# Loading half of chunk 0's w from another queue, r.(u k) of a third unit on TensorE, and a new order of all work, in a fused linear-attention and feed-forward kernel

## The chip, the cores and the metric

The kernel runs on one NeuronCore of a Trainium2 chip. The core has five engines with an instruction stream each: TensorE (PE in the profile) for matmuls and transposes, VectorE (DVE), ScalarE (ACT), GpSimd (POOL) and SyncE (SP), which here only issues transfers. Each engine works through its own instructions in order, and they wait for one another by semaphores. Transfers (DMA) are issued by SP and by GpSimd. The metric is the device time of one execution in microseconds (us), lower is better.

## What is computed

Two stages. The first is a linear attention with a decaying state, for 4 batches, 8 heads, 768 steps and head size 48; the second takes its output as 3072 tokens of 384 values through a feed-forward layer in which two products are multiplied.

```python
for t in range(S):
    kt, vt, rt, wt = (k[:, :, t], v[:, :, t], r[:, :, t], w[:, :, t])
    cur = np.einsum('bhd,bhe->bhde', u[None] * kt, vt)
    y[:, :, t] = np.einsum('bhd,bhde->bhe', rt, state + cur)
    state = wt[:, :, :, None] * state + np.einsum('bhd,bhe->bhde', kt, vt)
...
a = x @ w1            # x: 3072 x 384, w1 and w2: 384 x 1024
b = x @ w2
h = a * b @ w3        # w3: 1024 x 1024
return (h @ w_out).astype(np.float32)
```

All inputs and the output are float32.

## The kernel before

**Attention, by units.** The 768 steps are cut into six chunks of 128. A unit is one chunk of one or two batches; `UNITS` lists 13: unit 0 is chunk 0 of batch 0, unit 1 chunk 0 of batch 1, unit 2 chunk 0 of batches 2 and 3, and then two units of two batches for each of chunks 1 to 5. Within a unit (function `unit`, suffix `_t` on every name below) the recurrence is turned into matrix products: `ln` takes the logarithm of w (ACT, L670); `cs` and `ct` are its cumulative sums, in both layouts (TensorE, L679, L686); `ne` and `e` exponentiate them (ACT, L693, L699); `Kt` is k times the inverse decay (DVE, L704); `trr`/`RT` and `trk`/`KT` bring r and the decayed k into the transposed layout (TensorE L768 and L787, then DVE L773, and DVE or ACT L792); `m` is the product of both, `msk` its copy under the causal mask (DVE L812, or ACT L815 followed by a mask pass `maff` on GpSimd, L818); `y` multiplies by v (L850), `ys` adds the state's part (L841); `kv`, `T`, `S`, `Sc`, `Sb` bring the state on.

**The u term.** For each token and head it needs the number r.(u k), `dg`, which then multiplies v (`dv`, L750) and is added to y (`yb`, L862). It comes in one of two ways. Usually DVE or GpSimd multiplies r by k (`rk`, L709) and by u spread over all rows (`ruk`, L744), and DVE sums each head (`dg`, L748). For the units in `PE_DIAG`, TensorE sums: r k is transposed (`rkt`, L722), copied (`rke`, L727) and multiplied by `u_blk` (`d`, L736), a matrix with u in the rows of each head, and the result is copied (`dcp`, L741). `u_blk` is made once: two tiny matmuls from u (`ub`, L549 and L551), a DVE copy (`ublk`, L560) and two selects on GpSimd (`ublk2`, L564 and L566). `yt`/`xT` (L879, L884) transpose y for the second stage; units 9 to 12 do their transposes by DMA from SP.

**Feed-forward, by blocks.** `BLOCKS` joins units 0, 1 and 2 as blocks of their own, then two units each. Function `block` multiplies x by w1 and w2, some columns at a time (`a`, `b`, L939; b_0_1 is the second step of block 0, and steps 0 and 1 of blocks 0 and 1 need the first and second halves of the weights), copies a (`asb`, ACT L948), multiplies a by b (`abT`, DVE L952), and multiplies by `w34` (`o`, L961), which is w3 @ w_out, computed once in the kernel (`wt`, `wm`, L628 to L645). `osb` (L969) copies and SP stores.

**Loads.** Function `load` brings r, k, v and w of a unit (`rin`, `kin`, `vin`, `win`); r, k and v are cast to bfloat16 on the way, w stays float32. The loads in `SP_LOADS` are issued by SP, all others, the weights by `wload` too, by GpSimd.

**What sets the order.** Every piece of work is an `op` with an engine, an estimated duration and a key. The key is a base from the code, plus `RANK` of its kind, plus `STEP` of its name; where an op may run on two engines, `ENGINE` names the one. `schedule` plays the whole program through at build time with these estimates: whenever an engine is free it takes, among the ops that are ready by then, the one with the lowest key. The order so found is written out as each engine's instruction stream; on the chip nothing is chosen anew. An argument `late` makes the planner hold an op until others have ended, with no wait on the chip. Loads have keys near -10000, most other work between 59000 and 130000, so a load that the planner's model of the DMA queue lets through (`AHEAD`) goes ahead of GpSimd's other work.

Of the kernel before, what the change touches and what calls it, by code (L numbers as in the profile page):

```python
# [27 lines left out]
    "table": 113606.5, "ones": 79240, "LT": -1.5, "I128": 5.5, "pads": 139162.5, "rpads": 121276, "state0": 169505.5,  # L28
    "mask": 100743.5, "u": 3, "ub": 60310, "ubc": 114602.5, "ublk": 130965, "ublk2": 130038.5, "w1_0": -5,
    "w2_0": -3, "w1_1": -1, "w2_1": -13.5, "wo": -1, "w3_0": -4, "w3_1": -2, "w3_2": -1, "w3_3": -1, "gate": 23665.5,  # L30
    "wt_0": 171055.5, "w3Te_0": 170507.5, "wm_0": 33207, "w34e_0": 176250, "wt_1": 168598.5, "w3Te_1": 167528,
    "wm_1": 6037.5, "w34e_1": 178855, "wt_2": 170905, "w3Te_2": 175099, "wm_2": 5773.5, "w34e_2": 178246.5,
    "wt_3": 198481.5, "w3Te_3": 175459, "wm_3": 5604.5, "w34e_3": 178230, "wt_4": 198331.5, "w3Te_4": 174917.5,
    "wm_4": 32121, "w34e_4": 176157, "wt_5": 198774.5, "w3Te_5": 169927.5, "wm_5": 32634.5, "w34e_5": 178205.5,
    "wt_6": 198344, "w3Te_6": 176915, "wm_6": 5902.5, "w34e_6": 174984.5, "wt_7": 198309.5, "w3Te_7": 176726.5,
    "wm_7": 32627, "w34e_7": 178641.5, "rpad3": 113432.5, "win_0": 16, "kin_0": 2, "rin_0": 1, "vin_0": 3,
    "ln_0": 26693.5, "cs_0": 124632.5, "ct_0": 58880.5, "ne_0": 138927, "e_0": 171254, "Kt_0": 241553, "rk_0": 34358,
    "ruk_0": 85983, "dg_0": 5362.5, "dv_0": 114281, "trr_0": 155793, "RT_0": 111791.5, "trk_0": 127611,
    "KT_0": 146707.5, "m_0_0": 111506, "msk_0_0": 186441, "maff_0_0": 257875, "y_0": 144830.5, "yb_0": 253063,
# [135 lines left out]
BLOCKS = [[0], [1], [2], [3, 4], [5, 6], [7, 8], [9, 10], [11, 12]]
# [876 lines left out]
```

## Time and profile before

| what | value |
|---|---|
| median of 7 runs | 174.08 us (173.08 to 175.93) |
| the profiled execution | 173.16 us |
| its span, first to last instruction | 171.4 us |
| granted TensorE clock | 0.998 |
| TensorE busy | 153.9 us (90% of the span) |
| DVE, ACT, GpSimd busy | 120.5, 97.8, 108.7 us |
| bytes moved by DMA | 24.12 MB |

The durations in the views come from the one profiled execution; the 1.8 us between its time and its span lie before the first and after the last instruction. In a group of instructions the name of an output stands ahead of an arrow and its inputs behind it; after the count come busy time, mean duration in ns, and the engine's idle time just before these instructions with what ended it. A row of a stretch gives for each engine the busy time and, in brackets, the number of instructions. A row of a DMA issue ends with the size and the us from issue to landing. A row of waits names who waited, for whom, the total, the count and the longest.

### The profile page before, as it was taken

The page shows a single profiled execution, that of the slowest core. Times are in us where ns is not written, and L with a number is a line of the kernel's source. Part 1 is how long each engine was busy: PE and PEld are TensorE (multiplying, and loading weights), DVE is VectorE, ACT ScalarE, POOL GpSimd, SP SyncE. Part 2 cuts the span into 40 slices and gives each one's busy share as a digit, 9 for nine tenths or more (in the row PEclk, how much of TensorE's full clock was granted, in tenths as well). Part 3 has the DMA queues.
Part 4 walks back from the last instruction along what each step waited for, and adds up shares of the span by engine and source line. Part 5 has one row for each costly group of instructions (what it writes and reads, how often), then busy time and mean ns, then how long its engine had stood idle before and what let it go on. Part 6 is the DMA issues. An engine that isn't in the chain of part 4 may idle for free.

```text
span 171.4 us, 4130 instructions
## 1 busy us (share of the span) xinstructions
PE 153.9 (90%) x1711; PEld 98.6 (58%) x1726; DVE 120.5 (70%) x160; ACT 97.8 (57%) x130; POOL 108.7 (63%) x93
## 2 busy tenths in 40 slices
PE   0308799999999999999999999999999999999992
PEld 0206689998676765555756556655645455555560
DVE  5027888989888699999699697977976464231540
ACT  4512549887623785567987847875575643335101
POOL 7979698859799799999999969664142250000000
PEclk9999999999999999999999999999999999999999
DMA  6999999999989999999999998296145222211133
GB/s 102 143 161 183 175 244 172 163 206 173 208 196 142 189 165 137 191 216 144 162 169 257 203 100 155 76 145 181 28 90 100 96 46 48 96 46 46 46 111 121
DMA packets 98315, 24.12 MB, mean 141 GB/s; under 512 B 90680, under 2 KB 96312, under 8 KB 98296
## 3 DMA queue, kind: packets, MB, share of 16 engines
q0 software_dynamic: 78912, 15.47, 108.0%
q1 hardware_dynamic: 19384, 8.39, 21.1%
q8 instruction: 13, 0.21, 0.5%
q14 instruction: 6, 0.05, 0.1%
HBM read 27.79 MB, written 4.72 MB: 190 GB/s over the span
## 4 chain that ended last, share of the span: by engine, by line
PE 84%; DMA 4%; POOL 4%; DVE 3%; issue 2%; ACT 1%; POOLq 0%; ACTq 0%
PE banks L939 36%; PE banks L961 17%; PE banks L640 6%; DMA u_row<-in_u_dram 4%; PE banks L806 4%; PE banks L850 3%; PE banks L686 3%; PE banks L768 2%; PE banks L679 2%; PE banks L628 2%; PE banks L896 2%; PE banks L841 2%; PE banks L787 2%; PE banks L879 1%; POOL rin L580 1%
## 5 line engine op out<-in xcount | busy, mean ns | idle before, releaser
L939 PE MATMUL banks<-xT,w_bf 128*128 128x512 bf16 (+2 forms) x369 | 68.0, 326 | 1.0 <-ACT xT L884 0.3
L939 PEld LDWEIGHTS <-w_bf 128*128 128x128 bf16 x384 | 33.0, 99 | 24.7 <-issue 0.3
L952 DVE TENSOR_TENSOR abT<-a_sb,banks 128x1024 bf16<-128x1024 f32 (+1 forms) x28 | 29.8, 1066 | 19.4 <-PE banks L939 17.8
L948 ACT COPY a_sb<-banks 128x1024 f32<-128x1024 f32 (+1 forms) x28 | 25.0, 893 | 17.2 <-PE banks L939 15.0
L961 PE MATMUL banks<-w,abT 128*128 128x384 bf16 x192 | 34.3, 326 | 0.1
L818 POOL TENSOR_SCALAR_AFFINE_SELECT Mbf<-Mbf 128x1024 bf16<-128x1024 bf16 x16 | 17.4, 1094 | 13.1 <-ACT Mbf L815 13.1
L961 PEld LDWEIGHTS <-abT 128*128 128x128 bf16 x192 | 18.3, 98 | 12.4
L815 ACT CAST Mbf<-banks 128x1024 bf16<-128x1024 f32 x16 | 16.0, 1016 | 5.5 <-PE banks L806 5.5
L969 ACT COPY osb<-banks 128x384 f32<-128x384 f32 x14 | 6.7, 480 | 18.7 <-PE banks L961 18.6
L750 POOL TENSOR_TENSOR dv<-vin,dg 128x768 bf16<-128x768 bf16 (+1 forms) x9 | 12.6, 1406 | 7.1 <-DMA xT<-dv 3.7
L699 ACT ACTIVATE eT<-banks 128x1024 f32<-128x1024 f32 (+1 forms) x13 | 12.4, 957 | 5.7 <-PE banks L686 4.1
L704 DVE TENSOR_TENSOR Kt<-kin,banks 128x768 bf16<-128x768 bf16 (+1 forms) x11 | 9.5, 874 | 8.1 <-DMA kin<-in_k_dram 8.1
L862 DVE TENSOR_TENSOR dv<-banks,dv 128x768 bf16<-128x768 f32 (+1 forms) x13 | 11.6, 891 | 3.5 <-PE banks L850 3.2
L812 DVE TENSOR_TENSOR Mbf<-banks,mask 128x1024 bf16<-128x1024 f32 x8 | 9.8, 1220 | 3.8 <-PE banks L806 3.8
L686 PE MATMUL banks<-LT,lw 128*128 128x128 bf16 x96 | 8.3, 234 | 4.4 <-ACT lw L670 4.4
L709 POOL TENSOR_TENSOR rk<-rin,kin 128x768 bf16<-128x768 bf16 x6 | 9.8, 1641 | 2.5 <-DMA kin<-in_k_dram 2.5
L640 PE MATMUL banks<-wo_bf,w3T 128*128 128x384 bf16 x64 | 11.4, 327 | 0.0
L773 DVE TENSOR_TENSOR KRT<-banks,eT 128x1024 bf16<-128x1024 bf16 (+1 forms) x9 | 9.9, 1103 | 2.0 <-ACT eT L699 1.3
L670 ACT ACTIVATE lw<-win 128x768 bf16<-128x768 f32 (+1 forms) x11 | 8.6, 788 | 4.7 <-DMA win<-in_w_dram 4.4
L693 ACT ACTIVATE banks<-banks 128x768 f32<-128x768 f32 (+1 forms) x13 | 9.8, 752 | 2.4 <-PE banks L679 1.9
L787 PE MATMUL banks<-I,Kt 128*128 128x128 bf16 x64 | 5.0, 231 | 6.6 <-DVE Kt L704 6.6
L580 POOL DMA_DIRECT2D rin<-in_r_dram x7 | 10.0, 1423 | 1.0 <-POOLq L1036 0.8
(91 smaller groups left out, 239.6 us busy)
## 6 DMA issues: line engine op xcount, KB each, us to landing
out_dram<-osb SPq DMA_DIRECT2D x24, 192.0 KB, 2.2
win<-in_w_dram POOLq DMA_DIRECT2D x4, 768.0 KB, 9.2
w_bf<-in_moe_w_dram POOLq DMA_DIRECT2D x4, 512.0 KB, 9.9
w_bf<-in_moe_w_dram POOLq DMA_DIRECT2D x4, 384.0 KB, 7.8
rin<-in_r_dram POOLq DMA_DIRECT2D x4, 384.0 KB, 8.8
kin<-in_k_dram POOLq DMA_DIRECT2D x4, 384.0 KB, 8.6
vin<-in_v_dram POOLq DMA_DIRECT2D x4, 384.0 KB, 8.8
wo_bf<-in_moe_w_out_dram POOLq DMA_DIRECT2D x1, 768.0 KB, 9.5
```

What stands on the lines that cost most here:

```text
L580: op(eng, 60 if eng == "SP" else 650 + 270 * nb, lambda: e.dma_start(dst[:, b0 * H:(b0 + nb) * H, :D], ap), late=SP_ROWS if src == "w" and ...
L640: nc.tensor.matmul(o[:, :DM], lhsT=w3T[fi % 2][:, gi, :], rhs=wo_bf[:, gi, :], start=(gi == 0), stop=(gi == FI - 1))
L686: nc.tensor.matmul(o[:, b, q, :], lhsT=LW[:, b * H + 2 * q:b * H + 2 * q + 2, :].rearrange("t h d -> t (h d)"), rhs=LT, start=True, stop=True)
L699: nc.scalar.activation(ET[:, :, 1:], o[:, :nb * HP, :], Act.Exp)
L750: op("POOL", {"POOL": 100 + 1.8 * N, "DVE": dve(N)}, lambda e: ENG[e].tensor_mul(dvs, vv, dgs[:, :, None].to_broadcast([C, bh, D])), r=[f" ...
L815: nc.scalar.copy(Mbf[m].rearrange("s j q t -> s j (q t)"), banks[:, g.at(MM):g.at(MM) + 2, :])
L818: nc.gpsimd.affine_select(Mbf[m].rearrange("s j q t -> s (j q) t"), Mbf[m].rearrange("s j q t -> s (j q) t"), compare_op=Alu.is_gt, fill=0 ...
L862: nc.vector.tensor_add(ybs.rearrange("t b (q e d) -> t e (b q) d", e=2, d=D), o, dvs.rearrange("t (b q e) d -> t e (b q) d", b=nb, e=2))
L939: nc.tensor.matmul(o[:, q * T // TB, q % (TB // T), :], lhsT=wt[:, di, fi * P:(fi + 1) * P], rhs=xT[x][:, di, :T], start=(di == 0), stop=( ...
L948: nc.scalar.copy(a_sb[sa][:, :nbk * TB], banks[:, g.at(A):g.at(A) + nbk, :].rearrange("p k t -> p (k t)"))
L952: nc.vector.tensor_mul(abT[x][:, f[0]:f[0] + G, :T].rearrange("p i t -> p (i t)"), a_sb[sa][:, :nbk * TB], banks[:, g.at(Bk):g.at(Bk) + nb ...
L961: nc.tensor.matmul(banks[:, g.at(O), :DM], lhsT=abT[x][:, fi, tt * P:(tt + 1) * P], rhs=w34[:, fi, :], start=(fi == 0), stop=(fi == FI - 1))
```

## The change

`SP_LOADS` loses w of unit 2: SP issues w of units 0 and 1 (half of chunk 0's w), GpSimd that of unit 2. `PE_DIAG` gains unit 0. `RANK`, `STEP` and `ENGINE` are new throughout. The constants `WP` and `W3P` are written out as 2 and 4. The table lines below are those for the names that the prediction speaks of; nearly all other entries of the three tables are new as well.

```diff
RANK = {
...
-    "KT": -32021, "Kt": -126599, "RT": 12283, "S": 8478, "Sb": 24178, "Sc": 4497, "T": -63912, "a": -33006,
...
-    "dtk": 4456, "dtr": -30331, "dty": -11348, "dv": 2309, "e": -53690, "gate": -5921, "kv": -22477, "ln": 90720,
-    "m": -52126, "maff": -142053, "mask": 14517, "msk": -62096, "ne": -21947, "o": 72528, "ones": 38044,
...
-    "ubc": 2921, "ublk": -6276, "w34e": -51349, "w3Te": -50030, "wm": 55638, "wt": -109673, "xT": -151029,
...
+    "KT": -59002, "Kt": -156396, "RT": -9537, "S": 9698, "Sb": 4105, "Sc": -1961, "T": -74202, "a": -28563,
...
+    "dtk": 11195, "dtr": -35356, "dty": -11734, "dv": 8664, "e": -47925, "gate": -16883, "kv": -19093, "ln": 89439,
+    "m": -49493, "maff": -142402, "mask": 6933, "msk": -38393, "ne": -23481, "o": 80856, "ones": 46697,
...
}

STEP = {
-    "mask": 100743.5, "u": 3, "ub": 60310, "ubc": 114602.5, "ublk": 130965, "ublk2": 130038.5, "w1_0": -5,
-    "w2_0": -3, "w1_1": -1, "w2_1": -13.5, "wo": -1, "w3_0": -4, "w3_1": -2, "w3_2": -1, "w3_3": -1, "gate": 23665.5,
...
-    "wm_7": 32627, "w34e_7": 178641.5, "rpad3": 113432.5, "win_0": 16, "kin_0": 2, "rin_0": 1, "vin_0": 3,
...
-    "ruk_0": 85983, "dg_0": 5362.5, "dv_0": 114281, "trr_0": 155793, "RT_0": 111791.5, "trk_0": 127611,
...
-    "yt_0": 193451, "xT_0": 268468.5, "kv_0": 85387.5, "T_0": 178871.5, "S_0": 115755, "Sc_0": 117251.5,
...
-    "asb_0_1": 138945.5, "abT_0_1": 267085, "o_0_0": 16544.5, "osb_0_0": 176180, "store_0_0": 3021, "win_1": 5,
...
-    "abT_1_1": 266966.5, "o_1_0": 19075.5, "osb_1_0": 176211.5, "store_1_0": 6906, "win_2": 16, "kin_2": 3,
...
-    "Kt_2": 241604.5, "rk_2": 43019.5, "rkt_2": 123889, "rke_2": 155874, "d_2": 125422, "dcp_2": 43850,
-    "dv_2": 121048, "trr_2": 155377.5, "RT_2": 104841, "trk_2": 127526, "KT_2": 153183, "m_2_0": 112598,
-    "msk_2_0": 179172, "maff_2_0": 265178.5, "m_2_1": 111295.5, "msk_2_1": 179165.5, "maff_2_1": 265358.5,
...
+    "mask": 114325.5, "u": 6, "ub": 85613, "ubc": 115778.5, "ublk": 139994.5, "ublk2": 139582.5, "w1_0": -1,
+    "w2_0": -9, "w2_1": 1, "w3_0": -2, "w3_1": -1, "gate": 18300.5, "wt_0": 186936.5, "w3Te_0": 180388.5,
...
+    "rpad3": 110949.5, "win_0": 9, "kin_0": 2, "rin_0": 1, "vin_0": 7, "ln_0": 30931, "cs_0": 150610.5,
...
+    "rke_0": 160559, "d_0": 138446.5, "dcp_0": 35270, "dv_0": 113183, "trr_0": 168163.5, "RT_0": 130924.5,
...
+    "yb_0": 262883.5, "yt_0": 197545, "xT_0": 274692.5, "kv_0": 92018.5, "T_0": 197296, "S_0": 111557.5,
...
+    "store_0_0": 6002.5, "win_1": -4, "kin_1": -5, "rin_1": 3, "vin_1": 5, "ln_1": 30947, "cs_1": 150772,
...
+    "asb_1_1": 159555.5, "abT_1_1": 287058, "o_1_0": 5697.5, "osb_1_0": 183614.5, "store_1_0": 6383, "win_2": -2,
+    "kin_2": -10, "rin_2": -9, "vin_2": 4, "ln_2": 27502, "cs_2": 150899, "ct_2": 77090, "ne_2": 140677,
+    "e_2": 165156, "Kt_2": 277775, "rk_2": 8720.5, "rkt_2": 141179, "rke_2": 159467, "d_2": 138283.5, "dcp_2": 42304,
+    "dv_2": 112314.5, "trr_2": 168851, "RT_2": 128671.5, "trk_2": 151531.5, "KT_2": 175478, "m_2_0": 122874.5,
+    "msk_2_0": 157605, "maff_2_0": 263855, "m_2_1": 122898.5, "msk_2_1": 162959.5, "maff_2_1": 263536,
...
}

ENGINE = {
...
-    "w34e_5": "ACT", "w3Te_6": "ACT", "w34e_6": "DVE", "w3Te_7": "DVE", "w34e_7": "ACT", "rk_0": "DVE",
-    "ruk_0": "DVE", "dv_0": "DVE", "KT_0": "DVE", "msk_0_0": "DVE", "xT_0": "ACT", "S_0": "POOL", "osb_0_0": "DVE",
...
-    "msk_4_1": "DVE", "xT_4": "DVE", "S_4": "DVE", "osb_3_0": "DVE", "osb_3_1": "DVE", "osb_3_2": "ACT",
-    "osb_3_3": "ACT", "rk_5": "POOL", "ruk_5": "DVE", "dv_5": "DVE", "KT_5": "ACT", "msk_5_0": "ACT",
-    "msk_5_1": "ACT", "xT_5": "ACT", "S_5": "POOL", "rk_6": "DVE", "ruk_6": "POOL", "dv_6": "POOL", "KT_6": "DVE",
-    "msk_6_0": "ACT", "msk_6_1": "ACT", "xT_6": "ACT", "S_6": "POOL", "osb_4_0": "DVE", "osb_4_1": "DVE",
-    "osb_4_2": "ACT", "osb_4_3": "DVE", "rk_7": "DVE", "ruk_7": "DVE", "dv_7": "DVE", "KT_7": "ACT",
-    "msk_7_0": "ACT", "msk_7_1": "ACT", "xT_7": "ACT", "S_7": "POOL", "rk_8": "DVE", "ruk_8": "POOL", "dv_8": "POOL",
-    "KT_8": "ACT", "msk_8_0": "ACT", "msk_8_1": "DVE", "xT_8": "ACT", "S_8": "POOL", "osb_5_0": "ACT",
-    "osb_5_1": "ACT", "osb_5_2": "ACT", "osb_5_3": "ACT", "rk_9": "DVE", "ruk_9": "POOL", "dv_9": "POOL",
-    "msk_9_0": "DVE", "msk_9_1": "ACT", "Sb_9": "DVE", "rk_10": "DVE", "ruk_10": "DVE", "dv_10": "POOL",
...
+    "w34e_5": "DVE", "w3Te_6": "DVE", "w34e_6": "DVE", "w3Te_7": "ACT", "w34e_7": "ACT", "rk_0": "DVE",
+    "rke_0": "DVE", "dcp_0": "ACT", "dv_0": "DVE", "KT_0": "ACT", "msk_0_0": "DVE", "xT_0": "DVE", "S_0": "DVE",
+    "osb_0_0": "ACT", "rk_1": "DVE", "rke_1": "DVE", "dcp_1": "DVE", "dv_1": "POOL", "KT_1": "ACT", "msk_1_0": "DVE",
...
+    "msk_4_0": "ACT", "msk_4_1": "ACT", "xT_4": "ACT", "S_4": "DVE", "osb_3_0": "ACT", "osb_3_1": "ACT",
+    "osb_3_2": "DVE", "osb_3_3": "ACT", "rk_5": "POOL", "ruk_5": "DVE", "dv_5": "POOL", "KT_5": "DVE",
+    "msk_5_0": "DVE", "msk_5_1": "ACT", "xT_5": "ACT", "S_5": "POOL", "rk_6": "DVE", "ruk_6": "DVE", "dv_6": "POOL",
+    "KT_6": "ACT", "msk_6_0": "ACT", "msk_6_1": "DVE", "xT_6": "DVE", "S_6": "POOL", "osb_4_0": "ACT",
+    "osb_4_1": "ACT", "osb_4_2": "ACT", "osb_4_3": "DVE", "rk_7": "DVE", "ruk_7": "DVE", "dv_7": "POOL",
+    "KT_7": "ACT", "msk_7_0": "ACT", "msk_7_1": "ACT", "xT_7": "DVE", "S_7": "DVE", "rk_8": "DVE", "ruk_8": "POOL",
+    "dv_8": "DVE", "KT_8": "ACT", "msk_8_0": "ACT", "msk_8_1": "DVE", "xT_8": "ACT", "S_8": "DVE", "osb_5_0": "ACT",
+    "osb_5_1": "ACT", "osb_5_2": "ACT", "osb_5_3": "ACT", "rk_9": "POOL", "ruk_9": "DVE", "dv_9": "POOL",
+    "msk_9_0": "ACT", "msk_9_1": "ACT", "Sb_9": "POOL", "rk_10": "POOL", "ruk_10": "POOL", "dv_10": "POOL",
...
}
...
@@ -166,15 +167,13 @@
 DMA_KR = set(range(9, 13))
 DMA_Y = set(range(9, 13))
 DMA_R = set(range(9, 13))
-PE_DIAG = {1, 2}
+PE_DIAG = {0, 1, 2}
 
 WARM, FILL = 0.0, 0.0
 
-WP, W3P = 2, 4
-
 BLOCKS = [[0], [1], [2], [3, 4], [5, 6], [7, 8], [9, 10], [11, 12]]
 
-SP_LOADS = {("w", 0), ("w", 1), ("w", 2)}
+SP_LOADS = {("w", 0), ("w", 1)}
 
 CAPS = {"f": 4, "q": 6, "o": 2}
 
@@ -590,15 +589,15 @@
     w1r = moe_w1.rearrange("(di dp) f -> dp di f", dp=P)
     w2r = moe_w2.rearrange("(di dp) f -> dp di f", dp=P)
     wor = moe_w_out.rearrange("(gi gp) o -> gp gi o", gp=P)
-    FH, FQ = DFF // WP, FI // W3P
-    for h in range(WP):
+    FH, FQ = DFF // 2, FI // 4
+    for h in range(2):
         f = slice(h * FH, (h + 1) * FH)
-        wload(w1_bf[:, :, f], w1r[:, :, f], f"w1_{h}", DM * DFF * 4 // WP)
-        wload(w2_bf[:, :, f], w2r[:, :, f], f"w2_{h}", DM * DFF * 4 // WP)
+        wload(w1_bf[:, :, f], w1r[:, :, f], f"w1_{h}", DM * DFF * 2)
+        wload(w2_bf[:, :, f], w2r[:, :, f], f"w2_{h}", DM * DFF * 2)
     wload(wo_bf, wor, "wo", DFF * DM * 4)
-    for h in range(W3P):
+    for h in range(4):
         f = slice(h * FQ, (h + 1) * FQ)
-        wload(w3_bf[:, f, :], w3r[:, f, :], f"w3_{h}", DFF * DFF * 4 // W3P)
+        wload(w3_bf[:, f, :], w3r[:, f, :], f"w3_{h}", DFF * DFF)
 
 
     turn, done = [], 0
@@ -620,7 +619,7 @@
     def w34_block(fi):
         pr = 250 + fi * 12
         T = g.bank(f"wt{fi}", 1, "s")
-        src = f"w3_{fi * W3P // FI}"
+        src = f"w3_{fi // 2}"
 
         def tr():
             o = banks[:, g.at(T), :].bitcast(BF).rearrange("p (g f) -> p g f", f=P)
@@ -939,9 +938,9 @@
                         nc.tensor.matmul(o[:, q * T // TB, q % (TB // T), :], lhsT=wt[:, di, fi * P:(fi + 1) * P],
                                          rhs=xT[x][:, di, :T], start=(di == 0), stop=(di == DI - 1))
             cost = mm(*[T] * (DI * G))
-            op("PE", cost, lambda K=A, f=fis: fill(K, w1_bf, f), r=xs + free + [f"w1_{fis[0] * WP // FI}"],
+            op("PE", cost, lambda K=A, f=fis: fill(K, w1_bf, f), r=xs + free + [f"w1_{fis[0] // 4}"],
                w=[A, f"ad{n}_{z}", f"a_sb{sa}"], prio=pr + fis[0], name=f"a_{n}_{z}")
-            op("PE", cost, lambda K=Bk, f=fis: fill(K, w2_bf, f), r=xs + free + [f"w2_{fis[0] * WP // FI}", f"ad{n}_{z}"],
+            op("PE", cost, lambda K=Bk, f=fis: fill(K, w2_bf, f), r=xs + free + [f"w2_{fis[0] // 4}", f"ad{n}_{z}"],
                w=[Bk, f"bd{n}_{z}"], prio=pr + fis[0] + 0.5, name=f"b_{n}_{z}")
 
             def aev(A=A, sa=sa):

```

## The prediction

> **What bounds the kernel now.** I read the profile's first part, then the busy time by stretch, then TensorE's waits. The profiled execution took 173.16 us: 171.4 us of span and 1.8 us around it. The median of the runs is 0.92 us above it; I work out the difference on the profiled execution and add it to the median.
>
> ```profile
> PE 153.9 (90%) x1711; PEld 98.6 (58%) x1726; DVE 120.5 (70%) x160; ACT 97.8 (57%) x130; POOL 108.7 (63%) x93
> ```
>
> ```profile
> 0.00:23.07 23.07, 10.03 (x106) 7.41 (x107) 11.78 (x34) 9.82 (x15) 18.94 (x26) 1.00 1.62 160
> 23.07:168.10 145.03, 143.84 (x1606) 91.22 (x1620) 108.68 (x128) 87.47 (x115) 89.76 (x68) 1.00 1.27 138
> ...
> 60.00:100.00 40.00, 39.34 (x415) 23.48 (x419) 35.75 (x40) 29.93 (x39) 37.30 (x27) 1.00 2.34 182
> ```
>
> In a row of stretches the columns are PE, weight loads, DVE, ACT, POOL, clock, DMA. From 23.07 us, where the first feed-forward matmul starts, to 168.1 us TensorE is busy for 143.84 of 145.03 us. What is not work is the 13.04 us of idle before 23.07 (23.07 less 10.03) and 3.3 us of last copy and store at the end. So the change can win only in the front; behind it a new order can hardly win and can easily lose.
>
> ```profile
> PE banks L787 <- DVE Kt L704: 6.6, 1, 6.6
> PE banks L686 <- ACT lw L670: 4.4, 1, 4.4
> ```
>
> ```profile
> win<-in_w_dram SPq DMA_DIRECT2D x2, 192.0 KB, 3.1
> win<-in_w_dram SPq DMA_DIRECT2D x1, 384.0 KB, 7.6
> kin<-in_k_dram POOLq DMA_DIRECT2D x2, 96.0 KB, 7.1
> u_row<-in_u_dram POOLq DMA_DIRECT2D x1, 0.8 KB, 7.3
> ```
>
> The front waits for data: k lands at 11.4 and 11.9 (issue plus the last column), and u at 14.8. GpSimd's loads land in order: r of unit 2 at 8.6, v of unit 2 at 10.7, the two k, r of unit 0 at 12.7, a half of w2 at 14.6, u 14.8, r of unit 1 15.3, v of unit 0 16.0. That is 0.5 to 0.8 us for 96 KB, 2.1 for 192 KB, 1.9 for a weight half.
>
> **Part 1: w of unit 2 goes to GpSimd.** SP loses one issue, GpSimd gains one of about 1.15 us (v of unit 2 has that size and that row). The new keys put it behind k of units 2 and 1, r of unit 2, k and r of unit 0, and half of w2; u, r of unit 1, v of unit 0 and w1 are behind it. The clause `late` only orders the planner: the half of w2 is issued at 6.76 while w of unit 2 lands at 9.5.
>
> [...] The row: w of unit 2 on SP took 7.6 us beside the other loads, against 3.1 for its half-size fellows that came first. [...] By the row, taking w of unit 2 as 2.2 us of queue (the 768 KB w of unit 3 lands 4.5 us behind its predecessor), u would land as late as 15.8. [...]
>
> **Part 2: r.(u k) of unit 0 on TensorE.** Removed: a DVE multiply (0.35) and a DVE reduce (0.54). Added: three transposes (half of the 0.44 us that six take), a DVE copy (0.42, the 128x512 row), three tiny matmuls (0.07), an ACT copy (0.17). The work on TensorE is +0.29 us. But it also adds a wait: d_0 needs u_blk, which GpSimd masks in two selects (0.53 + 0.22). By the keys these stand behind all the loads. GpSimd's issues from 1.32 us (0.9 for 96 KB, 1.15 for 192 KB, 1.73 for 768 KB, 0.75 for a weight, 0.55 for u, 0.3 for each of two selects on constants) sum to 16.5 at the end of v of unit 2. So u lands 14.8, matmuls 0.74, u_blk on DVE 15.7, selects to 17.3, d_0 17.6, its copy 17.8. Behind the selects on GpSimd stand the next loads (the second half of w2, k of unit 3); the loads already issued keep the DMA queue fed for over 8 us (w of unit 3 lands 12.8 us after its issue), so a select that waits costs them nothing.
>
> **The front's sum.** DVE is in order. Of the ready operations the lowest key goes first: Kt_2 (121.4 thousand), RT_2 (119.1) and msk_2_0 (119.2) are below dv_0 (121.8) and xT_0 (121.7). From 15.7: rk_1 0.36, RT_1 0.69, rke_1 0.42, T_0 0.35, msk_1 1.21, S_0 0.35, dcp_1 0.17, Kt_2 0.94, RT_2 1.21 gives 21.4; dv_0 1.04 and yb_0 0.56 give 23.0; msk_2_0 1.21 and xT_0 0.42 give 24.6. The first feed-forward matmul is then at 24.7, 1.6 us later than now. But TensorE has done more by then: 0.29 for unit 0, and transposes (0.45 + 0.44), masked products (0.66) and d_2 (0.13) of unit 2, together 1.97. Idle is 24.7 - 10.03 - 1.97 = 12.7 for 13.04, less 0.34; with the added 0.29 of work the front comes to **0.0**. Bounds: -2.7 if dv_0, yb_0 and xT_0 go ahead of the three of unit 2 (start at 21.3, work 11.3, idle 10.0), +1.0 if u lands at 15.8.
>
> **Part 3: the orders and engines found anew.** Written constants for WP and W3P change no instruction. The engine table does. For units 5 to 8, whose DVE work runs between 60 and 103 us, DVE gains: unit 5 +0.3 (KT 0.68 and msk 1.22 come, dv 1.6 goes), unit 6 +1.9, unit 7 -0.5, unit 8 +2.2, sum 3.9; output copies give back 1.1, net **+2.8**. GpSimd loses 4.1 there, ACT about 2.5. DVE is at 35.75 of 40 us, so it goes to some 38.5. This is the stretch where DVE already decides:
>
> ```profile
> 84.00:92.00 8.00, 7.60 (x81) 4.64 (x79) 8.00 (x9) 6.48 (x10) 7.64 (x5) 1.00 2.35 190
> ...
> PE banks L806 <- DVE Kt L704: 0.3, 1, 0.3
> ...
> 87.30 1.82 DVE L709 TENSOR_TENSOR rk<-rin,kin 128x768 bf16<-128x768 bf16 x1
> ...
> L709 DVE TENSOR_TENSOR rk<-rin,kin 128x768 bf16<-128x768 bf16 x3 | 4.4, 1456 | 0.0
> L709 DVE TENSOR_TENSOR rk<-w_bf 128x768 bf16<-128x768 bf16 x2 | 1.0, 555 | 0.2 <-DMA w_bf<-in_k_dram 0.2
> ```
>
> With DVE full, TensorE is at 7.60 where the neighbouring stretches have 7.95: 0.35 us in 8. Bounds for the added 2.8: 0 if it fits into DVE's 4.25 us of gaps, 2.8 if none of it does. I take the row: four more full stretches of eight, **+1.4**. More than 0 because the planner counts such a multiply of 768 columns on DVE at its short 0.55 us, while three of five took 1.46 on average (the row above): its order packs DVE tighter than DVE is.
>
> [...]
>
> Between 28 and 60 us DVE loses about 3 us of work (w34 copies go to ACT); TensorE has no idle there, so this is worth nothing. Units 9 and 10 get 4.1 us more GpSimd work; GpSimd idles 2.9 us at 110 and has 2.5 of 8 us busy from 116 on, so I price it at +0.3 (0 to +1.5): the transposes of y at 121 us come a little later. The tail keeps its last copy on ACT, 0.48, and its store: 0.
>
> **Sum.** 0.0 + 1.4 + 0.3 = +1.7: the profiled execution 174.9, the median **175.8**, 1.0% slower.
>
> **Rivals.**
> (a) *The front wins.* dv_0 and xT_0 go ahead of unit 2, and DVE's excess is absorbed: -2.7 and +0.4 give 171.8. For it: k and r of unit 0 land earlier, and DVE idles for 8.05 us before k lands today. Against it: u, which everything of unit 0 needs, does not come earlier, and two selects on GpSimd are now behind it. It decides from the point where the first feed-forward matmul starts before about 22.5 with the same work done.
> (b) *It cancels.* Front 0.0, and the DVE excess fits: 174.1. For it: DVE has 4.25 us of gaps in 60 to 100. Against it: these are short waits for TensorE and ACT (0.2 to 1.4), not one hole.
> (c) *Data late.* The second half of w2, landed at 14.6 now, comes behind w of unit 3 (4.5), half of w1 (2.0) and v of unit 2 (2.1), itself 1.9, counted from v of unit 1 at 18.6: 29.1. If b_0_1 is written right behind a_0_1 (24.7 + 2.0 = 26.7), TensorE, in order, stands for 2.4 us: 1.7 + 2.4 = 4.1, 178.2. Against it: unit 3's cumulative sums, and block 1, some 4 us of work, are ready to be put there.
>
> **Numbers.** A measurement of this kernel can tell about 1% from no change, that is 1.74 us. The forecast has 0.42, of which 0.24 lies over +1% and 0.18 within; (a) 0.27, 0.23 of it over 1% faster; (b) 0.12, all within; (c) 0.19, all slower. So faster 0.23, same 0.34, slower 0.43. The forecast's own range is 174.1 to 177.3 (DVE excess at 0 to 2.8). The range for 8 in 10 runs from 171.0, (a) with no excess at all, to 179.2, (c) with the late u.
>
> **What would show it.** Right: k of unit 1 landing near 8 us and u near 14.8; the selects on u_blk ending near 17.3; the first feed-forward matmul (on xT, w_bf) between 24 and 25.5 with some 12 us of TensorE work before it; DVE at 38 of 40 us or more in 60 to 100 and TensorE under 39 there. Wrong: that matmul before 22.5; DVE under 36.5 of 40 in that stretch; TensorE idle for over 1 us at 25 to 30 us, which is (c).

## The result, and the profile after

The changed kernel takes 172.04 us (24 runs, 171.18 to 173.42) where the kernel before takes 174.06 (59 runs); the ratio is **0.990 [0.988, 0.992]**, 1.0% faster (the range in brackets is the 95% interval, here and below). Ratios are worked out from undisturbed executions alone, so they are not the quotient of the two medians, and no figure is read from the profiled executions of e2 and h3, which were disturbed. The forecast was 175.8, 1.0% slower. The profiled execution of the changed kernel took 172.04 us with a span of 170.3 (before 173.16 and 171.4), so the span is 1.1 us shorter. The medians differ by 2.0 us: the profiled execution of the kernel before was 0.9 us faster than its median, so part of the gain stands in no profile read here, and the profiles can place 1.1 us of it only. Most line numbers of the changed kernel are one lower (L938 for L939).

Busy time by stretch, of the changed kernel; the columns are those of the same view before (PE, weight loads, DVE, ACT, POOL, clock, DMA):

```profile
0.00:24.89 24.89, 12.85 (x133) 9.76 (x134) 13.98 (x37) 9.98 (x17) 21.49 (x28) 1.00 1.54 172
24.89:167.04 142.15, 141.02 (x1587) 89.82 (x1599) 104.95 (x119) 87.74 (x118) 85.37 (x63) 1.00 1.36 137
60.00:100.00 40.00, 39.68 (x477) 24.99 (x481) 36.00 (x43) 28.86 (x38) 36.48 (x25) 1.00 2.62 179
84.00:92.00 8.00, 7.95 (x93) 4.90 (x93) 7.42 (x8) 6.15 (x8) 6.84 (x5) 1.00 1.67 233
```

Up to the first feed-forward matmul TensorE idles 24.89 - 12.85 = 12.04 us, 1.00 less than before. From 60 to 100 us it idles 0.32 us where it idled 0.66, and the stretch of 84 to 92, which had 7.60 us of TensorE work, has 7.95. These two differences, -1.0 and -0.34, and +0.2 elsewhere make the 1.1 us of span. TensorE's busy sum is the same (153.9 us in both), though 0.29 us of work was added to it.

TensorE's waits, changed kernel (who waited for whom: total, times, longest):

```profile
PE banks L685 <- POOL LT L502: 5.1, 1, 5.1
PE banks L786 <- DVE Kt L703: 2.7, 2, 1.4
PE banks L548 <- DMA u_row<-in_u_dram: 2.6, 1, 2.6
PE banks L805 <- DVE KRT L772: 0.5, 1, 0.5
PE banks L721 <- ACT KRT L791: 0.5, 1, 0.5
```

and two of the kernel before:

```profile
PE banks L850 <- DVE u_blk L560: 1.1, 1, 1.1
PE banks L549 <- DMA u_row<-in_u_dram: 0.7, 1, 0.7
```

The wait for k (`Kt`) fell from 6.6 to 2.7 us. Three things took part of that back: the first wait, 4.4 for the logarithm before, is 5.1, because GpSimd now builds its constant `LT` behind three loads (from 4.75 us) where it stood behind two (from 3.88); the wait for u rose from 0.7 to 2.6; and short waits of 0.2 to 0.5 came where one of 1.1, which the profile puts down to `u_blk`, went. The sum is the -1.0. The transfers, changed kernel (last columns: size, us from issue to landing):

```profile
win<-in_w_dram POOLq DMA_DIRECT2D x1, 384.0 KB, 7.2
...
kin<-in_k_dram POOLq DMA_DIRECT2D x2, 96.0 KB, 4.5
```

k of units 0 and 1 comes in 4.5 us for 7.1 before. The new order also issues the first of the two earlier, at about 2.6 us for 4.1, so the first `Kt` starts at 7.4 for 11.6. w of unit 2 itself is hardly quicker (7.6 before).

And DVE in 60 to 100 us, changed kernel, groups by shape (count, busy, mean ns of one):

```profile
L811 DVE TENSOR_TENSOR Mbf<-banks,mask 128x1024 bf16<-128x1024 f32 x3 | 3.6, 1214 | 0.0
...
L749 DVE TENSOR_TENSOR dv<-w_bf,dg 128x768 bf16<-128x768 bf16 x1 | 1.0, 957 | 0.0
...
L708 DVE TENSOR_TENSOR rk<-rin,kin 128x768 bf16<-128x768 bf16 x1 | 0.5, 548 | 0.0
```

The masks are three for one, as forecast. But the slow multiply (three at 1456 ns before) is left once, at 548 ns, and of two `dv` of 1.67 and 1.59 us one is left, at 0.96. Not all slow ones are gone: the `ruk` of unit 6, which came from GpSimd, takes 1.80 us, and 0.55 elsewhere. So DVE's sum rose by 0.25 us, to 36.00, and not by 2.8. GpSimd's sum fell by 0.8 us in this stretch, to 36.48, where 4.1 had been forecast; over 60 to 116 us it fell by 2.3, from 50.0 to 47.7.

A second profile of the same changed kernel (run f1 below) has a span of 169.6, 11.4 us of front idle and DVE at 37.72 in 60 to 100. Differences of 0.6 us of front idle, or of 1.7 us of DVE there, are therefore no finding from one profile; the verdicts below rest on the repeated times, and the profile says where. The front's change stands clear of this: the four profiles with the changed front (also f4 and h4 below) idle 11.1 to 12.0 us before 28 us, the four with the old one (also e3, f3 and h1) 12.5 to 13.0.

### The profile page after: what moved, and what is told of

Same layout as the page of the kernel before. It is cut to its first block, busy times and chain, and to the rows that moved or that the text cites. A ratio compares the mean times of both kernels' runs of the same rounds, so it can differ in the third digit from the quotient of the medians.

```text
span 170.3 us, 4133 instructions
## 1 busy us (share of the span) xinstructions
PE 153.9 (90%) x1716; PEld 99.6 (58%) x1732; DVE 118.9 (70%) x156; ACT 98.0 (58%) x134; POOL 106.9 (63%) x90
## 4 chain that ended last, share of the span: by engine, by line
PE 86%; POOL 4%; DMA 4%; issue 2%; DVE 2%; ACT 1%; POOLq 0%; DVEq 0%
PE banks L938 36%; PE banks L960 19%; PE banks L639 6%; PE banks L805 4%; DMA u_row<-in_u_dram 4%; PE banks L849 3%; PE banks L685 3%; PE banks L627 2%; PE banks L767 2%; PE banks L895 2%; PE banks L786 2%; PE banks L678 2%; POOL kin L579 2%; PE banks L878 2%; PE banks L840 1%
## 5 line engine op out<-in xcount | busy, mean ns | idle before, releaser
L938 PE MATMUL banks<-xT,w_bf 128*128 128x512 bf16 (+2 forms) x368 | 66.5, 323 | 0.9
L938 PEld LDWEIGHTS <-w_bf 128*128 128x128 bf16 x384 | 32.7, 98 | 25.3 <-issue 0.4
L951 DVE TENSOR_TENSOR abT<-a_sb,banks 128x1024 bf16<-128x1024 f32 (+1 forms) x28 | 29.7, 1067 | 22.5 <-PE banks L938 20.3
L968 ACT COPY osb<-banks 128x384 f32<-128x384 f32 x19 | 9.1, 479 | 20.0 <-PE banks L960 18.4
L817 POOL TENSOR_SCALAR_AFFINE_SELECT Mbf<-Mbf 128x1024 bf16<-128x1024 bf16 x12 | 13.0, 1094 | 9.0 <-ACT Mbf L814 8.9
L811 DVE TENSOR_TENSOR Mbf<-banks,mask 128x1024 bf16<-128x1024 f32 x12 | 14.6, 1220 | 5.1 <-PE banks L805 3.9
L814 ACT CAST Mbf<-banks 128x1024 bf16<-128x1024 f32 x12 | 12.1, 1016 | 5.4 <-PE banks L805 5.4
L698 ACT ACTIVATE eT<-banks 128x1024 f32<-128x1024 f32 (+1 forms) x13 | 12.5, 958 | 2.8 <-PE banks L685 2.8
L708 POOL TENSOR_TENSOR rk<-rin,kin 128x768 bf16<-128x768 bf16 x8 | 13.5, 1690 | 0.6 <-DMA rin<-in_r_dram 0.6
L861 DVE TENSOR_TENSOR dv<-banks,dv 128x768 bf16<-128x768 f32 (+1 forms) x13 | 11.6, 893 | 2.0 <-PE banks L849 1.6
L579 POOL DMA_DIRECT2D vin<-in_v_dram x7 | 10.0, 1425 | 3.7 <-issue 3.7
L639 PE MATMUL banks<-wo_bf,w3T 128*128 128x384 bf16 x64 | 11.4, 327 | 0.0
L579 POOL DMA_DIRECT2D kin<-in_k_dram x7 | 10.1, 1438 | 0.9 <-POOLq L1035 0.8
L685 PEld LDWEIGHTS <-lw 128*128 128x128 bf16 x96 | 6.8, 104 | 6.5 <-ACT lw L669 4.2
```

Source lines behind the costliest of these rows:

```text
L579: op(eng, 60 if eng == "SP" else 650 + 270 * nb, lambda: e.dma_start(dst[:, b0 * H:(b0 + nb) * H, :D], ap), late=SP_ROWS if src == "w" and ...
L639: nc.tensor.matmul(o[:, :DM], lhsT=w3T[fi % 2][:, gi, :], rhs=wo_bf[:, gi, :], start=(gi == 0), stop=(gi == FI - 1))
L685: nc.tensor.matmul(o[:, b, q, :], lhsT=LW[:, b * H + 2 * q:b * H + 2 * q + 2, :].rearrange("t h d -> t (h d)"), rhs=LT, start=True, stop=True)
L698: nc.scalar.activation(ET[:, :, 1:], o[:, :nb * HP, :], Act.Exp)
L708: op("DVE", {"DVE": dve(N, 2), "POOL": 1490}, lambda e: ENG[e].tensor_mul(rks, rr[:, :, :D], kk), r=[*kr, *kk_], w=[f"rk{s}"], prio=pr + 8 ...
L811: nc.vector.tensor_mul(Mbf[m].rearrange("s j q t -> s (j q t)"), o.rearrange("s j f -> s (j f)"), mask.rearrange("s q t -> s (q t)"))
```

## The experiments

The theory after the result had two halves. In the front: the earlier k, that is w of unit 2 off SP, is the gain (L, the load); its rival: it is the new order of the work around it (O). Behind the front, the forecast's own step, that DVE's extra work costs TensorE 1.4 us, against a rival that the new engines are a gain. In the diffs `move` puts ops elsewhere in the planned order and `SWAP` changes the engine of ops in place, so that nothing else is planned anew.

### Only the load put back (e1)

```diff
-lambda: e.dma_start(dst[:, b0 * H:(b0 + nb) * H, :D], ap)
+lambda: (nc.sync if (src, t) == ("w", 2) else e).dma_start(dst[:, b0 * H:(b0 + nb) * H, :D], ap)
```

> The changed kernel's order on every engine, with only the issue of w of unit 2 given back to SP (it goes out right behind the other two w). Theory L (the front gained because k and r of units 0 and 1 no longer share the DMA engines with w of unit 2): k lands 1 to 2 us later, TensorE's idle time before the first feed-forward matmul rises from 12.0 to about 13 us, ratio to the kernel before 0.995 or more. Theory O (the front gained by its order, unit 2's products being put into the wait for u): u lands when it did, the start of feed-forward stays within 0.3 us of 24.9 and the ratio stays at 0.990.

Measured: 172.61 us against 173.92, ratio 0.9937 [0.9909, 0.9964]. The waits and the front, this kernel:

```profile
PE banks L786 <- DVE Kt L703: 5.4, 2, 3.8
```

```profile
0.00:28.00 28.00, 14.89 (x176) 11.62 (x177) 17.23 (x41) 12.58 (x21) 22.04 (x29) 1.00 1.61 163
```

The front idles 13.1 us again, as before the change, and the wait for k doubles from 2.7 to 5.4. k of units 0 and 1 is issued at the same times as in the changed kernel and takes 7.1 us to land again, for 4.5: w of unit 2 on SP is what makes it late. In the changed order the load is worth about 0.4% of the 1.0%, just at what the intervals can tell; the other 0.6% is elsewhere.

### Only the load moved, in the old order (e2, e5)

```diff
 order = g.schedule(CAPS)
+move(["win_2"], "u"); move(["ln_2"], "ct_2")        # e2; win_2 issued by GpSimd
+move(["I128", "win_2"], "u"); move(["ln_2"], "ct_2") # e5
```

> The order of the kernel before, with only w of unit 2 issued by GpSimd just ahead of u, and its logarithm moved on ACT to just ahead of its first reader. Theory L: k lands near 8 to 9.5 instead of 11.4 and 11.9, TensorE idles about 1 us less in the front, ratio 0.994. Theory O: k lands earlier, but u does not, and the first feed-forward matmul stays at 23.1; ratio 1.000 within 0.003.

Measured: 174.27 us, ratio 0.9961 [0.9918, 1.0004]: unclear. In this order GpSimd builds the identity `I`, which k's transposes need, behind the moved load. So in e5 the identity was moved ahead as well:

> As the second experiment (the order of the kernel before, w of unit 2 issued by GpSimd ahead of u), but with the select that makes the identity matrix moved ahead of it as well: in the second experiment TensorE's transposes of k waited 5.8 us for that select, so the earlier k could not be used. Theory L: Kt and the transposes of k now start near 8 us, idle time before the first feed-forward matmul falls by 0.5 to 1 us, ratio 0.993 to 0.997. Theory O: u still lands at 15 and everything of unit 0 behind it is unmoved; the first feed-forward matmul stays at 23 to 24 and idle within 0.3 us of 13.0, ratio within 0.003 of 1.

Measured: 173.77 against 173.32, ratio 1.0027 [0.9996, 1.0058]: no gain. Waits, e5:

```profile
PE banks L686 <- POOL LT L503: 4.2, 1, 4.2
PE banks L787 <- DVE Kt L704: 3.7, 1, 3.7
PE banks L549 <- DMA u_row<-in_u_dram: 3.6, 1, 3.6
```

The wait for k falls by 2.9 us, from 6.6 to 3.7, and the wait for u rises by 2.9, from 0.7 to 3.6. In the old order the earlier k is only handed on to u. So neither half explains the front alone. In the changed kernel more work on k and r stands ahead of the matmul on u, and there the load pays its 0.4%; which part of the new order it needs was not tried apart.

### The sum on TensorE undone (e6)

```diff
-op rkt_0, rke_0, d_0, dcp_0      (left out of the order)
+nc.vector.tensor_mul(y, y, u_bc[:, None, :].to_broadcast([C, 1, DM]))   # ahead of T_0
+nc.vector.reduce_sum(dg[0][:, :H], x, axis=AX.X)
```

> The changed kernel's order with r.(u k) of unit 0 taken off TensorE: no transposes, copy, tiny matmuls of unit 0; instead DVE multiplies by u and reduces just ahead of T_0. The prediction's step (three transposes and matmuls cost TensorE 0.29 us, and DVE's 0.9 us less is hidden in its wait): TensorE's work falls by 0.3, DVE runs 0.5 us later from 17 us on, the first feed-forward matmul comes 0 to 0.5 us later, net within 0.3 us, ratio to before 0.989 to 0.993. Rival D (DVE is what carries the front, so its 0.9 us are all paid): feed-forward starts at 25.7, ratio 0.995.

Measured: 171.95 us, ratio 0.9920 [0.9889, 0.9950], the same as the changed kernel. Unit 0's sum on TensorE is worth nothing that can be measured.

### The tables with the old switches (e4)

```diff
-PE_DIAG = {0, 1, 2}
+PE_DIAG = {1, 2}
-SP_LOADS = {("w", 0), ("w", 1)}
+SP_LOADS = {("w", 0), ("w", 1), ("w", 2)}
```

> The new RANK, STEP and ENGINE with the old SP_LOADS and PE_DIAG, planned anew (the two ops of unit 0 that the new tables lack get keys beside their neighbours). Theory O: the tables alone give most of it, ratio 0.990 to 0.994. Theory L: without the moved load the front is as before, 13 us of idle, ratio 0.997 to 1.003.

Measured: 179.86 us, ratio 1.0359 [1.0307, 1.0411]. TensorE idles everywhere, 1.6 us in 28 to 60, where all the other profiles read here lose 0.2 or less. The keys fit the program they were found for, to the op. Planning anew with one switch turned says nothing of the switch, which is why all other runs keep the order found and edit it in place.

### Loads by need (e7), and u earlier (e8, f2)

```diff
+move(['kin_1','LT','kin_0','rin_0','I128','u','rin_1','vin_0','win_2','w1_0','w2_0','vin_1','rin_2','kin_2'], <first>)  # e7
+move(["ones"], "kin_1")                                                                                     # e7
+move(["u"], "w2_0")                      # e8
+move(["u", "rin_1", "vin_0"], "w2_0")    # f2
```

> The changed kernel's order on TensorE, DVE and ACT, with GpSimd's first loads put in the order of need: k of unit 1, k and r of unit 0, u, r of unit 1, v of unit 0, w of unit 2, both first halves of w1 and w2, v of unit 1, then r and k of unit 2. Theory L (the front waits for data in the order of their landing): u lands near 10, r of unit 1 and v of unit 0 near 11 to 12, the waits for u (2.6 us) and k (2.7) go, feed-forward starts at 21 to 22.5, ratio 0.975 to 0.985. Rival W (weights or k of unit 2, now later, take the place of u): TensorE waits for w1, w2 or Kt of unit 2 instead, ratio 0.988 to 0.995.

Measured: 173.72 us, ratio 1.0018 [0.9986, 1.0051]: the whole gain is lost. Yet TensorE's idle before 28 us is 11.9, no more than in the changed kernel. The timeline of TensorE in e7 shows what is lost (start, duration, count at the end):

```profile
25.46 2.74 PE L938 MATMUL banks<-xT,w_bf 128*128 128x128 bf16 x24
28.00 0.35 PE L735 MATMUL banks<-u_blk,rkT 128*128 128x8 bf16 x6
```

and the same in the changed kernel:

```profile
21.67 1.06 PE L786 MATMUL banks<-I,Kt 128*128 128x128 bf16 x8
22.52 0.53 PE L849 MATMUL banks<-vin,Mbf 128*128 128x48 bf16 x8
...
24.89 1.51 PE L938 MATMUL banks<-xT,w_bf 128*128 128x128 bf16 x24
26.24 0.29 PE L735 MATMUL banks<-u_blk,rkT 128*128 128x8 bf16 x6
```

From its start to that of the next group, the same 24 matmuls take 2.54 us in e7, 106 ns each, and 1.35 us, 56 ns each, in the changed kernel. No wait stands between them, and the granted clock of 0 to 28 us is 1.00 in both. TensorE runs at half pace at the start, until some 24.5 us in the changed kernel (there the eight of 21.67 still take 106 ns each) and until about 30 in e7 (there the twelve matmuls of the same kind at 29.75 take 72 ns each, and those from 31.40 on 56). In e7 k of unit 2 lands at 21 us and TensorE waits 1.6 us for it, where the changed kernel has no wait; whether this gap is what puts off the end of the half pace was not tried apart, and all of it is read from one execution. Its busy sum is 157.4 us for 154.5 in f1, with the same 1732 matmuls in the records: 2.9 of the 3.2 us by which its span is longer. Late weights, which would show as a wait for `w_bf`, are not among TensorE's waits.

> The changed kernel with only u moved: GpSimd issues it ahead of the half of w2, so ahead of w of unit 2 as well. Theory L: u lands at 11 to 12 for 15.1, TensorE's wait of 2.6 us at its matmul goes, but r of unit 1 lands at 15.3 as before and the selects on GpSimd stay behind the loads, so the gain is at most 0.5 us, ratio 0.987 to 0.990. Theory U (u alone carries the front): feed-forward starts 2 us earlier, ratio 0.980.

Measured: 171.59 us, ratio 0.9910 [0.9876, 0.9945]. Waits, e8:

```profile
PE banks L685 <- POOL LT L502: 5.1, 1, 5.1
PE banks L767 <- DMA rin<-in_r_dram: 2.8, 1, 2.8
PE banks L786 <- POOL I L506: 1.7, 1, 1.7
```

The 2.6 us for u are gone, and r of unit 1 takes their place with 2.8.

> The changed kernel's order, with u, r of unit 1 and v of unit 0 issued ahead of the half of w2. With u alone moved, TensorE waited 2.8 us for r of unit 1 instead of 2.6 for u. If the front waits only for whichever of these three is last, moving all three lowers the idle time of 0 to 28 us from 11.65 (u alone) to 10 to 11 and the time to 170.5 to 171.3. If the wait is handed on again (to the half of w2, 2 us later, or to the identity mask on GpSimd), the idle stays at 11.5 to 12 and the time at 171.5 to 172.

Measured: 171.66 us against 171.79 for the changed kernel on the same chip (f1). Now the wait is 3.4 us for the identity from GpSimd, and the front idles 11.5 us, within what two profiles of the changed kernel show (11.4 and 12.0). Each transfer drawn forward gives its wait to the next in line; no version tried here is measurably better than the changed kernel.

### The changed kernel again (f1)

> The changed kernel itself, as a base for the others of this call. Expected 172.0, ratio 0.990.

Measured: 171.79 us (171.28 to 172.03), ratio 0.9889 [0.9862, 0.9917].

### The engines of units 5 to 8 (e3, f4)

These two test the step of the forecast that was worth +1.4 us. e3 puts the twelve changed engines of units 5 to 8 into the old order; f4 puts the old engines into the changed order.

```diff
+SWAP = {'dv_5': 'POOL', 'KT_5': 'DVE', 'msk_5_0': 'DVE', 'ruk_6': 'DVE', 'KT_6': 'ACT', 'msk_6_1': 'DVE',
+        'xT_6': 'DVE', 'dv_7': 'POOL', 'xT_7': 'DVE', 'S_7': 'DVE', 'dv_8': 'DVE', 'S_8': 'DVE'}   # e3; f4 the reverse
+for o in order:
+    if o.name in SWAP: o.eng = SWAP[o.name]
```

> The order of the kernel before, with only the engines of the attention work of units 5 to 8 taken from the changed kernel, each op in its old place. The step of the prediction (an added 2.8 us or more of DVE work between 60 and 100 us costs TensorE 1.4 us): DVE at 38.5 of 40 us or more there, TensorE under 38.4 of 40, ratio 1.008. Rival G (the work fits because the DVE operations that GpSimd slowed are gone): DVE at 36 to 37.5 of 40, TensorE at 39.2 or more, ratio within 0.003 of 1.

Measured: 172.82 us against 173.92, ratio 0.9946 [0.9916, 0.9975]. Faster, where the step said 1.4 us slower, and by more than its rival G allowed. The stretch, e3:

```profile
60.00:100.00 40.00, 39.68 (x417) 23.59 (x421) 37.08 (x44) 27.26 (x36) 34.58 (x24) 1.00 2.36 182
```

DVE is fuller by 1.3 us than before, TensorE too, by 0.34; GpSimd has 2.7 us less.

> The reverse of the swap that was tried in the order of before: the changed kernel's order, with the twelve operations of units 5 to 8 put back on the engines of before, in place. If those engines are what won behind the front, the time goes up by 0.3 to 0.6% against the changed kernel (ratio 0.993 to 0.996 to before) and TensorE's idle in 60 to 100 us from 0.32 back to about 0.7. If the gain lies in the order, nothing moves (0.990).

Measured: 175.17 us against 171.79 for f1, 2.0% slower (ratio to before 1.0099 [1.0062, 1.0136]). The stretch of f1, then the stretches and the wait that is new of f4:

```profile
60.00:100.00 40.00, 39.81 (x481) 24.84 (x479) 37.72 (x43) 28.39 (x38) 36.79 (x26) 1.00 2.56 182
```

```profile
60.00:100.00 40.00, 38.20 (x433) 23.31 (x431) 32.98 (x37) 29.31 (x38) 36.65 (x26) 1.00 2.43 166
100.00:116.00 16.00, 15.80 (x179) 9.25 (x177) 11.69 (x14) 11.83 (x18) 14.81 (x11) 1.00 1.02 128
```

```profile
PE banks L851 <- POOL Mbf L819: 1.4, 2, 1.2
```

DVE has 3.0 to 4.7 us less to do than in the two profiles of the changed kernel, and TensorE idles 1.8 us for 0.2 to 0.3. The largest new wait is for masks that GpSimd finishes late. Of the 3.8 us by which f4's span is longer than f1's, some 1.0 stands in the front already, whose order is the same; the rest is lost between 75 and 91 us, where those waits are.

### Which of the twelve (f3, h1, h3, h4)

```diff
+SWAP = {'dv_5': 'POOL', 'dv_7': 'POOL'}                                  # f3, old order
+SWAP = {'ruk_6': 'DVE', 'S_7': 'DVE', 'dv_8': 'DVE', 'S_8': 'DVE',
+        'msk_5_0': 'DVE', 'msk_6_1': 'DVE'}                              # h1, old order
+SWAP = {'msk_5_0': 'ACT', 'msk_6_1': 'ACT'}                              # h3, changed order
+SWAP = {'ruk_6': 'POOL', 'S_7': 'POOL', 'dv_8': 'POOL', 'S_8': 'POOL'}   # h4, changed order
```

> The order of before, only the multiplies dv of units 5 and 7 given to GpSimd, in place. They took 3.26 us on DVE before. If the in-place swap of units 5 to 8 gained (ratio 0.9946) because these two long multiplies leave DVE, this gives most of it: 0.995 to 0.997, DVE in 60 to 100 us at 32.5 to 34. If the gain came from the other ten swaps, or GpSimd (37.3 of 40 us busy before) becomes what is waited for: 0.999 to 1.005.

Measured: 173.90 us, ratio 1.0016 [0.9991, 1.0042]: no gain. f3's stretch:

```profile
60.00:100.00 40.00, 39.18 (x416) 23.14 (x415) 32.77 (x37) 29.31 (x38) 39.45 (x28) 1.00 2.25 175
```

DVE is relieved by 3 us and TensorE has no use of it; GpSimd is at 39.45 of 40.

> The order of before, only the six swaps of units 5 to 8 that take work off GpSimd: ruk_6, S_7, dv_8, S_8 and the masks msk_5_0 and msk_6_1 go to VectorE (with a mask on VectorE GpSimd has no second half of it to do). VectorE gets about 5 us, GpSimd loses about 6.5. If GpSimd was what held the stretch: ratio 0.992 to 0.997, GpSimd in 60 to 100 us at 31 to 33 of 40, TensorE at 39.6 or more. If VectorE decides, as the prediction had it: VectorE at 38 to 39.5 there, TensorE under 39, ratio 1.005 to 1.015.

Measured: 173.33 us, ratio 0.9971 [0.9939, 1.0003]: probably a gain, with an interval that just reaches no change. h1's stretch:

```profile
60.00:100.00 40.00, 39.80 (x421) 23.42 (x420) 37.50 (x45) 27.72 (x36) 31.49 (x22) 1.00 2.39 182
```

Six operations more on DVE, and DVE at 37.50 rather than the 38 to 39.5 that the other theory wanted; TensorE at 39.80.

> The changed order, only the masks msk_5_0 and msk_6_1 back on ACT with their second half on GpSimd. With all twelve put back TensorE waited 1.4 us for such masks of GpSimd. If GpSimd's two halves (2.2 us) are what makes it late: ratio to before 0.994 to 1.000 (0.5 to 1% slower than the changed kernel), and the wait for a mask of GpSimd is back. If the multiplies are: 0.989 to 0.992.

Measured: 173.49 us, ratio 0.9977 [0.9946, 1.0008], some 0.8% slower than the changed kernel by its 0.990.

> The changed order, only ruk_6, S_7, dv_8 and S_8 back on GpSimd, 4.8 us of its work. If GpSimd's load as such is the cause: ratio to before 0.997 to 1.005, GpSimd full between 68 and 108 us. If the masks alone are the cause: 0.989 to 0.992.

Measured: 173.69 us, ratio 1.0000 [0.9969, 1.0031], some 1.0% slower than the changed kernel. h4's stretch:

```profile
60.00:100.00 40.00, 38.38 (x453) 23.39 (x451) 33.74 (x38) 27.79 (x36) 38.04 (x28) 1.00 2.48 171
```

In the changed order the masks' 0.8% and the multiplies' 1.0% come near the 2.0% of all twelve. Both load GpSimd and relieve DVE, and both lose. Over these kernels TensorE is fullest where DVE is full (39.68 and 39.80 us at 37.08 and 37.50 of DVE) and emptier where DVE has little (39.18, 38.20 and 38.38 at 32.77, 32.98 and 33.74): DVE's sum was the wrong thing to watch. GpSimd's sum orders them no better (36.65 in f4, 36.79 in f1); f4's new wait is for two masks of it that come late. e3's gain is clear of noise and by f3 is not DVE's relief; h1, which relieves GpSimd alone, has about half of it, and not clear of noise; f4, h3 and h4 lose, but they also take from the new order the engines it was planned for, a rival that was not tried apart. So GpSimd as the engine to relieve is the likely reading, and not shown by itself. What the other six swaps add was not tried either, and since each order was found for its own engines, 0.5% in the one and 2.0% in the other can't be added to the front's share.

## Why the prediction was wrong

- **Part 1, the load: right in its times.** k of unit 1 was forecast near 8 us (its `Kt` starts at 7.4), u at 14.8 (15.1, and 14.4 in f1; by the row of w on SP it would have been 15.8). The 14.8, where u landed before, stands in the sum as the author's estimate: no run shows that u must land there again. What the runs show is 15.1 and 14.4, and that the queue which issues w of unit 2 matters to k: k of units 0 and 1 takes 4.5 us with that load on GpSimd and 7.1 with it on SP (e1).
- **Part 2, the sum on TensorE: right.** The selects on `u_blk` were to end at 17.3 and ended at 17.0; nothing waits for them, and by e6 the edit is worth nothing that can be measured.
- **The front's sum: its time came out by luck.** First feed-forward matmul forecast 24.7, measured 24.89 (23.81 in f1), but not by the line of DVE work that the forecast added up. DVE's timeline of the changed kernel, and one line of TensorE's:

```profile
19.85 0.95 DVE L703 TENSOR_TENSOR Kt<-kin,banks 128x768 bf16<-128x768 bf16 x1
20.73 0.55 DVE L749 TENSOR_TENSOR dv<-vin,dg 128x384 bf16<-128x384 bf16 x1
...
21.98 1.23 DVE L772 TENSOR_TENSOR KRT<-banks,eT 128x1024 bf16<-128x1024 bf16 x1
23.41 0.36 DVE L883 COPY xT<-banks 128x384 bf16<-128x384 bf16 x1 [0.20 <-PE banks L878]
...
25.00 1.23 DVE L811 TENSOR_TENSOR Mbf<-banks,mask 128x1024 bf16<-128x1024 f32 x1 [0.97 <-PE banks L805]
```

```profile
23.83 0.80 PE L721 MATMUL banks<-I,rk 128*128 128x128 bf16 x6 [0.46 <-ACT KRT L791]
```

  `Kt_2` went first as forecast, but then `dv_0` ahead of `RT_2`, and `xT_0` ahead of `msk_2_0`; `dv_0` took 0.55 us for 1.04. So `xT_0` was done at 23.8, not 24.6. What then held the matmul was TensorE's own order: transposes of r k of unit 2, behind a wait of 0.5 us for ACT, and products of unit 2 stand ahead of it.

  One term was also too small. TensorE had done 12.85 us of work by then, not 12.0: k's eight transposes of unit 2 were put at 0.45 and the six of r k at 0.44, and they take 0.85 and 0.73 us, start to next start (the eight are in the timeline of the changed kernel under e7). The small values are those of full pace; these stand ahead of 24.5 us, at half. Idle was so 12.0, not 12.7, and the front won 1.0 where 0.0 was forecast. The wait for k fell by 3.9 us and the others rose by 2.8, and the prediction had seen this shape: u "does not come earlier".
- **Part 3, the step that failed: "+1.4" for DVE's excess of 2.8 us in 60 to 100 us.** This step is 1.7 of the 2.8 us between forecast (+1.7) and profile (-1.1); the front is 1.0. DVE's excess was 0.25 us (2.0 in f1), TensorE's idle there fell by 0.34 us, and the change of engines wins: -0.5% in the old order (e3), and +2.0% when it is undone in the new (f4). The prediction took the full DVE of 84 to 92 us as DVE's own load. In that stretch `dv` took 1.59 us and `rk` 1.82, which take 0.96 (the `dv` of the same shape at 86.89 of the changed kernel) and 0.55 us (the next `rk`, at 90.79) elsewhere, so, by the author's estimate, 1.9 of the 8.00 us were no work of DVE's. Beside the first GpSimd runs a multiply (85.69 to 86.55), as it does beside the one of 2.00 us in the last section; beside the second it issues a transfer, and whether that holds DVE isn't settled: the two `rk` of 0.555 us in the prediction's row stood beside such an issue too (74.05 to 75.08). Its own row had GpSimd at 37.30 of 40, above DVE's 35.75, and it wrote "GpSimd loses 4.1 there", but its bounds for this stretch began at 0. The bound from below should have let this term be negative.
- **Units 9 and 10, +0.3:** TensorE idles 0.06 us more in 100 to 116 us, and 0.1 more behind it; small and of the right sign.
- **Its signs for being wrong.** "DVE under 36.5 of 40" did happen in the first profile (36.00) and not in the second (37.72), so it wasn't a safe sign; "TensorE under 39 there" failed in both (39.68, 39.81). Rival (c), late data at 25 to 30 us, did not come. Rival (a) had the right size, 171.8, and in part the right order on DVE, but not its front: the first feed-forward matmul was not before 22.5.
- **Two sums of its ranges.** (a) without any excess is 174.1 - 2.7 = 171.4, not 171.0, and a DVE excess of 2.8 with the 0.3 of units 9 and 10 gives 177.2, not 177.3.

## What to carry to other kernels

Before calling an engine full, take each of its long instructions at its undisturbed length from another row: what is left over may be waiting that the profile counts as work (here 1.9 of 8.00 us). Look for the engine that holds it up: relieving that one may be worth more than the work it hands over costs. When a transfer comes earlier, ask which wait is next in line, and judge the load and the order together. To test one switch of a planned program, edit the order that was found, since a new plan with old keys measures the keys.

## What the runs showed of the hardware that was not expected

**A DVE multiply of two SBUF tensors took 2.00 us beside a multiply on GpSimd, and 0.55 elsewhere.** GpSimd's and then DVE's timeline of the kernel before:

```profile
61.42 1.64 POOL L709 TENSOR_TENSOR rk<-rin,kin 128x768 bf16<-128x768 bf16 x1
```

```profile
61.49 2.00 DVE L709 TENSOR_TENSOR rk<-rin,kin 128x768 bf16<-128x768 bf16 x1
...
85.79 1.59 DVE L750 TENSOR_TENSOR dv<-w_bf,dg 128x768 bf16<-128x768 bf16 x1
87.30 1.82 DVE L709 TENSOR_TENSOR rk<-rin,kin 128x768 bf16<-128x768 bf16 x1
```

GpSimd starts 0.07 us ahead and ends at 63.06; DVE ends at 63.49, 0.43 us later, where the same multiply takes 0.55 at 90.79, so, by the author's estimate, it did next to nothing meanwhile. It is the longest of the three in the 1456 ns row. The `ruk` of 1.80 us in the changed kernel looks the same: it starts at 68.11 and ends 0.42 us after a GpSimd multiply of 68.63 to 69.49. What keeps DVE there, no run shows. Whether a transfer's issue on GpSimd does the same is not settled: the multiplies at 74.05, 75.00 and 90.79 stood beside one and took 0.55 us each, and the one at 87.30, which starts during one, 1.82.

**One instruction of one program took 0.55 us in one execution and 2.37 in another.** DVE's timeline of the changed kernel, in its second profile (f1):

```profile
92.55 2.37 DVE L906 TENSOR_TENSOR Sst<-Tst,eT 128x384 f32<-128x384 f32 x1
```

and in its first:

```profile
93.62 0.55 DVE L906 TENSOR_TENSOR Sst<-Tst,eT 128x384 f32<-128x384 f32 x1
```

In the first it starts 0.03 us ahead of GpSimd's next instruction, a transfer's issue at 93.65. In the second that issue began 0.92 us before it, a mask follows on GpSimd until 94.49, and the multiply ends 0.43 us after the mask. The mask alone can't be it: from 92.55 an undisturbed multiply would have ended at 93.10, before the mask began at 93.39. Whether the issue holds it, here but not elsewhere, isn't settled. A shift of 0.95 us between two engines thus adds 1.82 us to DVE, about the whole 1.7 by which its sum in 60 to 100 us differs between the two executions.

**The half pace of the start is not in the granted clock.** That clock is 1.00 over 0 to 28 us, while matmuls of 128 columns take 106 ns each at 21.67 us of the changed kernel and 56 at 24.89. The slower pace ends by 26 us at the latest in the kernel before, the changed kernel (f1 too), e1, e3 to e6, e8 and h4, and at about 30 in e7; what ends it was not tried apart. Work drawn ahead of that point costs up to twice what the rows behind it show (106 ns for 56); in e7 the later end came with 2.9 us of longer matmuls.
